# Transposing the attention output on TensorE in every unit, and storing the result in natural token order

## The chip, the core and the metric

The kernel runs on one NeuronCore of a Trainium2 chip. The metric is the device time in microseconds (us) of one execution, the median of repeated runs. Profile times are microseconds from the first instruction of the profiled execution.

## The reference

A gated linear attention with a decay per key channel, and after it a two-layer network with a squared relu. Inputs are float32; q, k, v and alpha are 4 batches x 8 heads x 768 tokens x 48 channels, the weights 384 x 2048 and 2048 x 384.

```python
state = zeros((B, H, D, D))
for t in range(S):
    state = alpha[:, :, t, :, None] * state + einsum('bhd,bhe->bhde', k[:, :, t], v[:, :, t])
    y[:, :, t] = einsum('bhd,bhde->bhe', q[:, :, t], state)
x = y.transpose(0, 2, 1, 3).reshape(B * S, H * D)      # 3072 x 384
h = x @ w_in
r = maximum(h, 0.0)
out = (r * r) @ w_out                                    # 3072 x 384, float32
```

## The kernel before

The 768 tokens of a batch are cut into three pieces of 256, so there are 12 units (g = 0 to 11), ordered piece by piece over the four batches. A unit goes through these steps, named here as the text below uses them, with the lines of the profile:

- **load** (L477): four transfers (alpha, k, q, v; 384 KB each) issued on SP's queue. Partition p holds the tokens 2p and 2p+1 of the unit, the two under an index j.
- **front**: the product of the two alphas (L493/L495), its logarithm (L496), cumulative sums on TensorE (L504 to L508, called m1), exponentials (L516 to L526), and scaled k and q in bf16 (`qks`, L542). Then q and k are transposed to `kqt`: on TensorE for units 0 to 2 (L556), and by a transposing transfer issued on SP's queue for units 3 to 11 (L569, one for k and one for q).
- **back**: the state update (L587, called kv), the scores (L625, one group of 16 matmuls into psX and one into psZ), the mask (L631), the attention output in psX (L645 and L652, called y), its copy to bf16 (`xbf`, L662 on ScalarE or L664 on VectorE). Then `xbf` is transposed to `xt`: for units 0 to 2 by six TensorE transposes into psX (L674) and a copy out (L680 or L682); for units 3 to 11 by a transposing transfer on SP's queue (L685).
- **moe**: the first layer in 8 groups of 6 matmuls (L712, called s1), each into one of two PSUM banks psH; a relu of each group to `rr` (L719 on ScalarE, L721 on VectorE) and a square to `gt` (L725, L728); the second layer as two tiles of 128 tokens with 16 matmuls each, cut into groups of 4 (L738, called s2), into the one bank psO; a copy out to `osb` (L745), and the store (L751).

Rows of `y` stand with j outside: partition 64j + s of half c is the token 2(64c + s) + j. That order goes through `xt`, `rr` and `gt` to the rows of `osb`, so each tile of 128 output rows is stored by two transfers of 64 rows, each to every second row of the output.

The order of every engine is fixed beforehand by a list scheduler in the kernel (`Program.schedule`): each operation has a cost in ns, a priority and dependencies, DMA transfers share the bandwidth by a table of weights, and the operation with the smallest priority among those that are ready goes next. Some operations have alternatives on other engines. The engines then run their lists strictly in that order and wait on semaphores; SP's list holds every load, every transposing transfer and every store. At the beginning, while TensorE has no work, matmuls on zeros are put in (L784).

Of the kernel before, what the change touches and what calls it, by code (L numbers as in the profile page):

```python
# [6 lines left out]
ALU = mybir.AluOpType  # L7
AF = mybir.ActivationFunctionType
# [25 lines left out]
class Program:  # L34
# [6 lines left out]
    RING = {"sp": 24.0, "act": 20.0, "pool": 130.0}  # L41
# [55 lines left out]
    def schedule(self):  # L97
# [9 lines left out]
        rings = {"sp": [], "act": [], "pool": []}  # L107
# [206 lines left out]
def act_ns(n):  # L314
    return 180 + n * 0.8333
# [10 lines left out]
def bass_gla_recurrent__then__act_relu_squared_kernel(  # L326
# [10 lines left out]
    HD = H * D  # L337
# [11 lines left out]
    PE_X = 3  # L349
# [110 lines left out]
    load_op = {}  # L460

# [3 lines left out]
    def load(g):  # L465
        b, i = units[g]
        t0 = i * T
        p0 = g * P
        r, la, qs, kt, pm, vb, x2 = (g % n for n in (NRAW, 2, NQKS, NKQT, NPM, NV, 2))
        first, last = i == 0, i == NST - 1  # L470
        xt = XSLOT[g]
        sr, sw = 2 * b + i % 2, 2 * b + (i + 1) % 2

        for j, t, nm in ((0, alpha, "a"), (1, k, "k"), (2, q, "q"), (3, v, "v")):
            src = t[b, :, t0:t0 + T, :].rearrange("h (p j) d -> p h (j d)", j=2)
            dst = RAW[r][:, j].rearrange("p h j d -> p h (j d)")
            load_op[g, nm] = add("sp", lambda e, dst=dst, src=src: e.dma_start(dst, src), 400, L_PRIO[g] + j,  # L477
                writes=[("raw", r, j)], name=f"ld{nm}{g}", dma=f"{nm}{r}", lag=1230,
                after=[load_op[AFTER[g]]] if g in AFTER else [])

    def front(g):
# [39 lines left out]
        if not last:  # L521
# [15 lines left out]
        vin, vout = RAW[r][:, 3].rearrange("p h j d -> p (h j d)"), VBF[vb][:].rearrange("p h j d -> p (h j d)")  # L537
        add("pool", lambda e: e.tensor_copy(vout, vin), 830, p0 + 900, reads=[("raw", r, 3)], writes=[("vbf", vb)],  # L538
            name=f"vc{g}", alts={"act": (lambda e: e.activation(vout, vin, AF.Copy), act_ns(2 * HD))})
# [8 lines left out]
        for a in range(2):  # L548
# [18 lines left out]
            else:  # L567
                dst = KQT[kt][:, a].rearrange("p j n s -> p (j n) s")
                add(TR_RING, lambda e, dst=dst, src=src: e.dma_start_transpose(dst, src), 500, p0 + 2500 + a,  # L569
                    reads=[("qks", qs, a)], writes=[("kqt", kt, a)], name=f"tr{a}_{g}", dma=f"t{a}_{kt}", lag=1250)  # L570

    def back(g):
# [111 lines left out]
        else:  # L684
            add(TR_RING, lambda e: e.dma_start_transpose(dst, src), 500, p0 + 6700, reads=[("xbf", x2)],  # L685
                writes=[("xt", s, slot)], name=f"xt{g}", dma=f"x{s}{slot}", lag=950)
# [5 lines left out]
    def moe(m, gs):  # L692
# [8 lines left out]
        for u in range(nb):  # L701
# [5 lines left out]
            def s1(pe, u=u, hb=hb):  # L707
# [11 lines left out]
            add("act", lambda e, hb=hb, rb=rb: e.activation(RR[rb][:], psH[hb][:], AF.Relu), act_ns(512), pu + 600,  # L719
                reads=[("ps", "H", hb)], writes=[("rr", rb)], name=f"re{m}_{u}",  # L720
                alts={"dve": (lambda e, hb=hb, rb=rb: e.tensor_scalar(RR[rb][:], psH[hb][:], 0.0, None, ALU.max),  # L721
# [7 lines left out]
        for ti, (ui, jq) in enumerate((ui, jq) for ui in range(nu_) for jq in range(2)):  # L729
# [18 lines left out]
            for j in range(2):  # L748
                r0 = b * S + i * T + 128 * jq + j
                dst = bass.AP(tensor=out.tensor, offset=out.offset + r0 * DM, ap=[[2 * DM, 64], [1, DM]])  # L750
                add("sp", lambda e, ob=ob, dst=dst, j=j: e.dma_start(dst, OSB[ob][64 * j:64 * j + 64, :]), 500,  # L751
                    ps_ + 1300, reads=[("osb", ob)], name=f"out{m}_{ti}_{j}", dma=f"o{ob}{j}", lag=300)
# [10 lines left out]
    for g in range(5, G):  # L763
# [3 lines left out]
             ("wout", 1): (2, "a"), 3: ("wout", 0), 4: ("wout", 0), 5: ("wout", 1), 6: ("wout", 1)}  # L767
# [48 lines left out]
```

## Time and profile before

| | |
|---|---|
| time, median of 3 runs (lowest to highest) | 194.6 us (194.4 to 195.27) |
| the profiled execution's own time | 195.71 us |
| its span, first to last instruction | 194.0 us |
| mean granted TensorE clock | 0.987 |
| busy: TensorE / weight loads / VectorE / ScalarE / GpSimd | 176.8 / 126.2 / 119.4 / 118.9 / 32.0 us |
| hardware DMA queue | 79,968 packets, 30.09 MB |

A row of the timeline gives the start, the length, the engine (PE is TensorE, DVE VectorE, ACT ScalarE, POOL GpSimd, SPq the queue of SyncE), the line, the operation with output<-input, and in brackets the idle time of that engine just ahead and what ended it. The chain of waits is followed back from the last instruction: start, length, what. The table of stretches gives for each stretch the busy time of the engines with their instruction counts, the granted clock of TensorE, the share of the DMA engines and GB/s.

### The profile page before, as it was taken

The numbers are of one execution on the slowest core, as the hardware profiler recorded it, in microseconds if no ns is written. First come the engines' busy times: TensorE is split into PE (matmuls) and PEld (weight loads), VectorE is DVE, ScalarE is ACT, GpSimd is POOL, SyncE is SP. The second block draws the span as 40 slices with busy tenths as digits, with TensorE's granted clock in tenths as the row PEclk, the third lists the DMA queues.
The fourth block names the chain that finished last, engine by engine and source line by source line (L and its number), as shares of the span: only waits on it lengthen the run. The fifth ranks groups of instructions, "written<-read, shape, count | busy, mean of one in ns | idle before, by whom it ended". The sixth has DMA issues, their size and how long they took to land.

```text
span 194.0 us, 5232 instructions
## 1 busy us (share of the span) xinstructions
PE 176.8 (91%) x2255; PEld 126.2 (65%) x2255; DVE 119.4 (62%) x204; ACT 118.9 (61%) x217; POOL 32.0 (16%) x40
## 2 busy tenths in 40 slices
PE   7998995999898949689999999999999999999980
PEld 5767883666574537357777668667777676677740
DVE  6698886676778738651983984929819427144210
ACT  3575796366768247916876768568757564466511
POOL 3061140105022324400300331301000101000000
PEclk9999999999999999969999999999999999999998
DMA  5999999989999999999899998562633440321211
GB/s 160 325 260 200 258 200 194 216 206 316 157 319 192 291 194 256 208 268 272 199 293 300 185 251 186 80 129 46 130 80 79 98 81 3 78 47 30 51 41 41
DMA packets 82870, 33.56 MB, mean 173 GB/s; under 512 B 76960, under 2 KB 82080, under 8 KB 82848
## 3 DMA queue, kind: packets, MB, share of 16 engines
q1 hardware_dynamic: 79968, 30.09, 68.7%
q0 software_dynamic: 2880, 3.15, 10.0%
q8 instruction: 17, 0.28, 0.6%
q14 instruction: 5, 0.04, 0.1%
HBM read 25.17 MB, written 4.72 MB: 154 GB/s over the span
## 4 chain that ended last, share of the span: by engine, by line
PE 62%; DMA 23%; ACT 4%; SPq 3%; DVE 2%; POOL 2%; issue 1%
PE psO L738 28%; PE psH L712 25%; DMA raw<-in_alpha_dram 12%; DMA wout<-in_moe_w_out_dram 5%; DMA win<-in_moe_w_in_dram 4%; DMA xt<-xbf 3%; PE psX L652 2%; PE psX L645 2%; PE psZ L587 2%; POOL prd L495 2%; SPq L477 2%; PE psX L625 1%; SPq L569 1%; PE psW L504 1%; PE psZ L625 1%
## 5 line engine op out<-in xcount | busy, mean ns | idle before, releaser
L712 PE MATMUL psH<-xt,win 128*128 128x256 bf16 x576 | 73.8, 274 | 5.7 <-DMA xt<-xbf 4.8
L738 PE MATMUL psO<-wout,gt 128*128 128x384 bf16 x384 | 73.1, 329 | 2.6 <-DMA wout<-in_moe_w_out_dram 2.1
L712 PEld LDWEIGHTS psH<-xt,win 128*128 128x128 bf16 x576 | 54.0, 98 | 18.0 <-DMA xt<-xbf 2.9
L719 ACT ACTIVATE rr<-psH 128x512 bf16<-128x512 f32 x84 | 49.9, 596 | 25.7 <-PE psH L712 24.1
L725 DVE TENSOR_TENSOR gt<-rr 128x512 bf16<-128x512 bf16 x66 | 28.8, 443 | 41.8 <-ACT rr L719 41.5
L738 PEld LDWEIGHTS psO<-wout,gt 128*128 128x128 bf16 x384 | 36.2, 98 | 23.3 <-DMA wout<-in_moe_w_out_dram 2.2
L745 ACT ACTIVATE osb<-psO 128x384 f32<-128x384 f32 x24 | 11.8, 491 | 22.7 <-PE psO L738 22.3
L728 ACT ACTIVATE gt<-rr 128x512 bf16<-128x512 bf16 x30 | 18.7, 626 | 1.3 <-DVE rr L721 0.8
L603 POOL TENSOR_TENSOR smd<-tmp,own 128x384 bf16<-128x384 f32 x7 | 7.4, 1057 | 56.2 <-DVE tmp L601 56.2
L631 DVE TENSOR_TENSOR pm<-psZ,caus 128x1024 bf16<-128x1024 f32 x12 | 14.6, 1217 | 1.7 <-PE psZ L625 1.7
L631 DVE TENSOR_TENSOR pm<-psX,caus 128x1024 bf16<-128x1024 f32 x12 | 14.6, 1217 | 0.9 <-PE psX L625 0.8
L721 DVE TENSOR_SCALAR rr<-psH 128x512 bf16<-128x512 f32 x12 | 8.3, 689 | 8.8 <-PE psH L712 8.7
L784 PE MATMUL psO<-zero 128*128 128x256 bf16 x77 | 12.0, 302 | 1.3 <-DVE zero L411 1.3
L662 ACT ACTIVATE xbf<-psX 128x768 bf16<-128x768 f32 x10 | 8.1, 810 | 6.9 <-PE psX L652 6.9
L542 DVE TENSOR_TENSOR qks<-raw,ek 128x768 bf16<-128x768 f32 x12 | 11.5, 955 | 0.4 <-POOL ek L528 0.2
L542 DVE TENSOR_TENSOR qks<-raw,eq 128x768 bf16<-128x768 f32 x12 | 11.4, 951 | 0.1
L496 ACT ACTIVATE lab<-prd 128x384 bf16<-128x384 f32 x12 | 6.2, 520 | 7.4 <-POOL prd L495 5.8
L784 PEld LDWEIGHTS psO<-zero 128*128 128x128 bf16 x77 | 8.0, 108 | 3.2 <-DVE zero L411 1.2
L610 POOL TENSOR_TENSOR sbd<-tmp,acm 128x384 bf16<-128x384 f32 x8 | 7.0, 870 | 18.0 <-DVE tmp L608 18.0
L495 POOL TENSOR_TENSOR prd<-raw 128x384 f32<-128x384 f32 x4 | 5.1, 1268 | 21.4 <-DMA raw<-in_alpha_dram 21.4
L538 POOL CAST vbf<-raw 128x768 bf16<-128x768 f32 x5 | 4.5, 891 | 21.4 <-DMA raw<-in_v_dram 17.7
L534 DVE TENSOR_TENSOR eq<-eq,raw 128x384 f32<-128x384 f32 x12 | 7.9, 657 | 0.0
(75 smaller groups left out, 145.8 us busy)
## 6 DMA issues: line engine op xcount, KB each, us to landing
raw<-in_alpha_dram SPq DMA_DIRECT2D x12, 384.0 KB, 3.9
raw<-in_k_dram SPq DMA_DIRECT2D x12, 384.0 KB, 4.4
raw<-in_q_dram SPq DMA_DIRECT2D x12, 384.0 KB, 5.0
raw<-in_v_dram SPq DMA_DIRECT2D x12, 384.0 KB, 5.2
out_dram<-osb SPq DMA_DIRECT2D x48, 96.0 KB, 2.3
win<-in_moe_w_in_dram POOLq DMA_DIRECT2D x2, 768.0 KB, 9.4
wout<-in_moe_w_out_dram POOLq DMA_DIRECT2D x2, 768.0 KB, 11.3
kqt<-qks SPq DMA_TRANSPOSE x18, 3.9
```

The lines of the kernel that those rows point to most:

```text
L495: alts={"pool": (lambda e: e.tensor_tensor(hd(PRD[la][:]), al(0), al(1), ALU.mult), pool_ns(HD))})
L542: add("dve", lambda e, a=a, E=E: e.tensor_tensor(QKS[qs][:, a, :, :, 0:D], RAW[r][:, 1 + a].rearrange("p h j d -> p j h d"), E[la][:].rear ...
L631: add("dve", lambda e, hf=hf, psT=psT: e.tensor_tensor(PM[pm][:, hf].rearrange("p r n j t -> p (r n) (j t)"), psT[:, :, :].rearrange("p r ...
L662: add("act", lambda e: e.activation(XBF[x2][:], psX[:, :, 0:HD], AF.Copy), act_ns(2 * HD), p0 + 6100, reads=[("ps", "X", 0), ("ps", "X", 1 ...
L712: ins = pe.matmul(psH[hb][:, i * n:(i + 1) * n], WIN[:, kk, fj * 128:(fj + 1) * 128], mov, start=(kk == 0), stop=(kk == KT - 1))
L719: add("act", lambda e, hb=hb, rb=rb: e.activation(RR[rb][:], psH[hb][:], AF.Relu), act_ns(512), pu + 600, reads=[("ps", "H", hb)], writes= ...
L721: alts={"dve": (lambda e, hb=hb, rb=rb: e.tensor_scalar(RR[rb][:], psH[hb][:], 0.0, None, ALU.max), dve_ns(512))})
L725: add("dve", lambda e, dst=dst, sq=sq: e.tensor_tensor(dst, sq, sq, ALU.mult), 415, pu + 1200, reads=[("rr", rb)], writes=[("gt", gt, g0 + ...
L728: "act": (lambda e, dst=dst, sq=sq: e.activation(dst, sq, AF.Square), act_ns(512))})
L738: ins = pe.matmul(psO[:, 0:DM], GT[gt][:, fj, g0 + ui, jq, :], WOUT[:, fj, :], start=(fj == 0), stop=(fj == FT - 1))
L745: add("act", lambda e, ob=ob: e.activation(OSB[ob][:], psO[:, 0:DM], AF.Copy), act_ns(DM), ps_ + 700, reads=[("ps", "O")], writes=[("osb", ...
L784: pr.fill(lambda pe: pe.matmul(psO[:, 0:256], ZERO[:, 0:128], ZERO[:, 0:256], skip_group_check=True), 109, min(o.start for o in pr.order[" ...
```

## The change

Four things are edited.

1. `PE_X` goes from 3 to the number of units: in all 12 units the six TensorE transposes into psX and a copy out make `xt`; the nine transposing transfers of L685 are gone.
2. The relu writes `rr` permuted: it reads psH as before and writes each element to its place with the token's j innermost, so consecutive elements of a run land 4 bytes apart. `rr`, `gt` and the output rows are then in natural token order.
3. The store of a tile is one transfer of 128 consecutive rows instead of two of 64.
4. The scheduler's description of the DMA is another: weights by kind of transfer in place of weights by queue, longer issue costs of transposing transfers and stores. Code for loads on another queue is added, with a constant that leaves all loads on SP (`SW_LOADS = G`), and entries of the table `AFTER` are taken out for units 4 to 6, which the next line of the code overwrites in both kernels.

```diff
-    RING = {"sp": 24.0, "act": 20.0, "pool": 130.0}
+    PACKET = (("win", 172), ("wout", 79), ("ld", 22), ("tr", 18), ("xt", 18), ("out", 65))
...
         def rates():
-            total = sum(self.RING[r] for r, q in rings.items() if q)
-            return {r: self.RING[r] / total for r, q in rings.items() if q}
+            took = {r: next(t for n, t in self.PACKET if q[0].name.startswith(n)) for r, q in rings.items() if q}
+            return {r: t / sum(took.values()) for r, t in took.items()}
...
-    PE_X = 3
+    PE_X = G
...
+    SW_LOADS = G
...
-                add(TR_RING, lambda e, dst=dst, src=src: e.dma_start_transpose(dst, src), 500, p0 + 2500 + a,
-                    reads=[("qks", qs, a)], writes=[("kqt", kt, a)], name=f"tr{a}_{g}", dma=f"t{a}_{kt}", lag=1250)
+                add(TR_RING, lambda e, dst=dst, src=src: e.dma_start_transpose(dst, src), 1300, p0 + 2500 + a,
+                    reads=[("qks", qs, a)], writes=[("kqt", kt, a)], name=f"tr{a}_{g}", dma=f"t{a}_{kt}", lag=1700)
...
-            add("act", lambda e, hb=hb, rb=rb: e.activation(RR[rb][:], psH[hb][:], AF.Relu), act_ns(512), pu + 600,
+            rin = psH[hb][:].rearrange("p (x j t) -> p x j t", j=2, t=64)
+            rout = RR[rb][:].rearrange("p (x t j) -> p x j t", j=2, t=64)
+            add("act", lambda e, rin=rin, rout=rout: e.activation(rout, rin, AF.Relu), act_ns(512), pu + 600,
...
-            for j in range(2):
-                r0 = b * S + i * T + 128 * jq + j
-                dst = bass.AP(tensor=out.tensor, offset=out.offset + r0 * DM, ap=[[2 * DM, 64], [1, DM]])
-                add("sp", lambda e, ob=ob, dst=dst, j=j: e.dma_start(dst, OSB[ob][64 * j:64 * j + 64, :]), 500,
-                    ps_ + 1300, reads=[("osb", ob)], name=f"out{m}_{ti}_{j}", dma=f"o{ob}{j}", lag=300)
+            r0 = b * S + i * T + 128 * jq
+            add("sp", lambda e, ob=ob, r0=r0: e.dma_start(out[r0:r0 + 128, :], OSB[ob][:]), 600, ps_ + 1300,
+                reads=[("osb", ob)], name=f"out{m}_{ti}", dma=f"o{ob}", lag=600)
```

With other operations and costs the scheduler writes other lists. On TensorE the two lists are the same, row for row but for one matmul on zeros, up to the first group of s1 matmuls ahead of unit 3's scores. The first place is the end of unit 4's back in the kernel before: the second group of scores of unit 4, its y, and the first s1 groups of unit 3.

```order
L625 MATMUL psZ<-kqt 64x128 x16
L738 MATMUL psO<-wout,gt 128x384 x4
L504 MATMUL psW<-lab,linc 128x384
L506 MATMUL psW<-hcol,hsel 128x8
L508 MATMUL psW<-ones,lab 128x2 x4
L645 MATMUL psX<-sbd,kqt 64x96 x8
L645 MATMUL psX<-smd,kqt 64x96 x8
L652 MATMUL psX<-vbf,pm 128x48 x32
L712 MATMUL psH<-xt,win 128x256 x12
```

In the changed kernel (line numbers are those of its own file: L651/L658 is y, L593 kv, L718 s1, L747 s2, L680 the transposes of `xbf`) unit 3's first s1 group is the last row here, before any score of unit 4:

```order
L651 MATMUL psX<-smd,kqt 64x96 x8
L658 MATMUL psX<-vbf,pm 128x48 x32
L593 MATMUL psZ<-vbf,qks 128x96 x16
L718 MATMUL psH<-xt,win 128x256 x6
L509 MATMUL psW<-lab,linc 128x384
L511 MATMUL psW<-hcol,hsel 128x8
L513 MATMUL psW<-ones,lab 128x2 x4
L680 MATMUL psX<-ident,xbf 128x128 x6
L747 MATMUL psO<-wout,gt 128x384 x4
L718 MATMUL psH<-xt,win 128x256 x6
```

So s1 of unit 3 has moved from behind y of unit 4 to a few groups behind y of unit 3; when unit 4's scores begin, three more s1 groups, two more s2 groups and one group of transposes have been issued than before. The transposes stand one or two groups behind y in the later units too. The second place is SP's list, from the loads of unit 6 on; before:

```order
L477 DMA raw<-in_v_dram 128x8x96
L685 DMA_TRANSPOSE xt<-xbf 128x6x128
L569 DMA_TRANSPOSE kqt<-qks 128x8x128
L751 DMA out_dram<-osb 64x384 x2
L569 DMA_TRANSPOSE kqt<-qks 128x8x128
L477 DMA raw<-in_alpha_dram 128x8x96
```

and in the changed kernel:

```order
L482 DMA raw<-in_v_dram 128x8x96
L575 DMA_TRANSPOSE kqt<-qks 128x8x128
L758 DMA out_dram<-osb 128x384
L575 DMA_TRANSPOSE kqt<-qks 128x8x128
L482 DMA raw<-in_alpha_dram 128x8x96
```

The transfer of `xbf` is gone from between the loads of unit 6 and the transposing transfers of unit 5, and the store is one row.

More of the change, by code (lines that the diff above doesn't have):

```diff
@@ L472, in load @@
         sr, sw = 2 * b + i % 2, 2 * b + (i + 1) % 2
+        ring, cost = ("sp", 600) if g < SW_LOADS else ("pool", 930)
         for j, t, nm in ((0, alpha, "a"), (1, k, "k"), (2, q, "q"), (3, v, "v")):
             src = t[b, :, t0:t0 + T, :].rearrange("h (p j) d -> p h (j d)", j=2)
-            dst = RAW[r][:, j].rearrange("p h j d -> p h (j d)")
-            load_op[g, nm] = add("sp", lambda e, dst=dst, src=src: e.dma_start(dst, src), 400, L_PRIO[g] + j,
-                writes=[("raw", r, j)], name=f"ld{nm}{g}", dma=f"{nm}{r}", lag=1230,
+            dst, key = RAW[r][:, j], ("raw", r, j)
+            if nm == "v" and ring == "pool":
+                dst, key = VBF[vb], ("vbf", vb)
+            dst = dst[:].rearrange("p h j d -> p h (j d)")
+            load_op[g, nm] = add(ring, lambda e, dst=dst, src=src: e.dma_start(dst, src), cost, L_PRIO[g] + j,
+                writes=[key], name=f"ld{nm}{g}", dma=f"{nm}{r}{ring}", lag=1230,
                 after=[load_op[AFTER[g]]] if g in AFTER else [])
@@ L684, in back @@
         else:
-            add(TR_RING, lambda e: e.dma_start_transpose(dst, src), 500, p0 + 6700, reads=[("xbf", x2)],
-                writes=[("xt", s, slot)], name=f"xt{g}", dma=f"x{s}{slot}", lag=950)
+            add(TR_RING, lambda e: e.dma_start_transpose(dst, src), 1300, p0 + 6700, reads=[("xbf", x2)],
+                writes=[("xt", s, slot)], name=f"xt{g}", dma=f"x{s}{slot}", lag=1400)
     rr_i = [0]
```

11 lines of the change are left out of this document (6 added, 5 removed).

## The prediction

> **What bounds the kernel now.** First the table of stretches (after the span and its length: TensorE, weight loads, VectorE, ScalarE, GpSimd, then the granted clock, the DMA share and GB/s).
>
> ```profile
> 50.00:60.00 10.00, 9.11 (x135) 6.68 (x134) 8.06 (x11) 7.34 (x15) 2.00 (x2) 1.00 1.22 262
> 60.00:70.00 10.00, 7.13 (x128) 4.06 (x126) 7.30 (x11) 5.14 (x11) 2.54 (x3) 1.00 1.12 237
> 70.00:80.00 10.00, 8.41 (x107) 6.24 (x108) 6.11 (x10) 6.38 (x12) 3.45 (x4) 1.00 0.99 246
> 80.00:90.00 10.00, 7.96 (x89) 5.13 (x88) 3.45 (x5) 4.48 (x10) 1.81 (x2) 0.83 1.13 244
> ...
> 100.00:180.00 80.00, 79.97 (x1005) 57.52 (x1004) 47.09 (x78) 51.19 (x91) 8.24 (x8) 1.00 0.56 116
> ```
>
> From 100 to 180 TensorE has no gap: whatever it does there, it does back to back, and only less work or an earlier start can end it sooner. Between 50 and 90 it is idle 0.89 + 2.87 + 1.59 + 2.04 = 7.4 us, and in the last ten of these the clock was granted at 0.83. So the question is what ends the gaps there. TensorE's own timeline names it:
>
> ```profile
> 53.29 0.42 PE L625 MATMUL psX<-kqt 64*64 64x128 bf16 x16 [0.76 <-DMA kqt<-qks]
> ...
> 63.36 0.42 PE L625 MATMUL psX<-kqt 64*64 64x128 bf16 x16 [1.26 <-DMA kqt<-qks]
> ...
> 71.36 1.48 PE L712 MATMUL psH<-xt,win 128*128 128x256 bf16 x12 [2.81 <-DMA xt<-xbf]
> ...
> 82.95 1.39 PE L712 MATMUL psH<-xt,win 128*128 128x256 bf16 x6 [2.04 <-DMA xt<-xbf]
> ```
>
> The two long ones are s1 of units 3 and 4, waiting for the transposing transfer that the change removes. The two short ones are scores waiting for transfers that stay. Why `xt` is late stands in VectorE's row for `xbf` of unit 3 and in SP's timeline:
>
> ```profile
> 58.10 0.95 DVE L664 CAST xbf<-psX 128x768 bf16<-128x768 f32 x1
> ```
>
> ```profile
> 51.38 0.58 SPq L477 DMA_DIRECT2D raw<-in_alpha_dram  x1
> ...
> 59.51 1.85 SPq L569 DMA_TRANSPOSE kqt<-qks  x1
> 61.41 0.58 SPq L477 DMA_DIRECT2D raw<-in_alpha_dram  x1
> ...
> 65.46 2.06 SPq L685 DMA_TRANSPOSE xt<-xbf  x1
> 67.57 1.31 SPq L569 DMA_TRANSPOSE kqt<-qks  x1
> ...
> 70.76 1.36 SPq L569 DMA_TRANSPOSE kqt<-qks  x1
> ```
>
> `xbf` is ready at 59.05, but its transfer is issued at 65.46, behind the transposing transfer of unit 4 and the four loads of unit 6 on SP, and lands just before 71.36: 12.3 us, of which 6.4 are queueing.
>
> **The change part by part.** Prices at full clock come from the chain of waits, where TensorE runs without gaps:
>
> ```profile
> 43.21 0.34 PE psX L674 x6
> ...
> 90.95 0.16 PE psW L504
> 91.12 0.45 PE psZ L587 x16
> ...
> 92.98 0.65 PE psO L738 x4
> 93.63 1.31 PE psH L712 x12
> ...
> 96.89 0.35 PE psX L625 x16
> 97.24 0.22 PE psZ L625 x16
> ...
> 100.84 0.46 PE psX L645 x16
> 101.30 0.51 PE psX L652 x32
> ```
>
> *How much can be won at all.* From 53.29 to 82.95 are 29.66 us. The list of the kernel before has in them 78 s1 matmuls (6.5 x 1.31 = 8.5), 44 of s2 (11 x 0.65 = 7.15), three units' scores (3 x 0.57 = 1.7), two y (one without its state half: 1.8), two kv (0.9) and the m1 parts (five of 0.16 and their small matmuls, about 1.1): 21.2 us. The same count over the gapless stretch from 89.64 to 186.04 falls 4% short of its 96.4 us, so 0.85 of the missing 8.5 us is the price of any stretch; 7.6 are lost. Ahead of 53.29 come 0.76. Behind 82.95 the clock is still low:
>
> ```profile
> 82.95 1.39 PE psH L712 x6
> 84.34 1.28 PE psO L738 x4
> 85.62 0.78 PE psX L645 x16
> ```
>
> This is 3.45 us for what costs 0.655 + 0.65 + 0.46 = 1.77: 1.7 lost. In all 10.1 us is the ceiling of the gain.
>
> *Does it go?* In the changed list `xt` of unit 3 is made right behind its y. With `xbf` at about 59, transposes 0.34 and the copy out, s1 of unit 3 is free at about 60.5 instead of 71.3. Ahead of unit 4's scores the list now has three s1 groups (1.96), two s2 groups (1.3) and the transposes (0.34): 3.6 us of work, against the 1.26 us in which these scores waited, while the transfers they wait for are issued no later (59.51 for the second). Unit 3's scores get one s1 and one s2 group more ahead of them, 1.3 us for a wait of 0.76, and begin at about 53.8. Behind them TensorE has 3.5 us of s1, s2 and m1 to do while VectorE masks unit 4. So both `xt` waits and both `kqt` waits have cover. If it fails, unit 4's scores wait at most their old 1.26 us. Next in line are unit 5's scores: their two transfers were issued at 67.57 and 70.76; without the 2.06 us of `xt` ahead of them and with one store issue less they go out by about 65.5 and 68.5, land by 72.5 (the median below), and the list needs them at 53.8 + 20.9 = 74.7, with 19.6 us of work and 1.3 us for its ends between. From there each unit costs TensorE about 13.6 us, against 10.0 us from the alpha load of unit 5 (51.38) to that of unit 6 (61.41) on SP, so loads no longer come last. Small waits for the logarithm (about 0.5 in sum) stay. I take -9.6 us, bounds -4.9 (the two idle times alone) and -10.1.
>
> The clock's loss is in this sum only because it follows a gap. The Trainium skill's page TensorE: Matmul & The Clock Gate (What's actually happening) has the clock halve after an idle window of some 3.4 us that runs freely. The trace agrees in part: 2.04 us of idle ending at 82.95 brought 0.83, yet the 2.81 us ending at 71.36 left 1.00.
>
> ```profile
> out_dram<-osb SPq DMA_DIRECT2D x48, 96.0 KB, 2.3
> ...
> kqt<-qks SPq DMA_TRANSPOSE x18, 3.9
> ```
>
> *Transposes.* Nine units x 0.34 = +3.1 us, on the engine that sets the end. Each waits for `xbf`, and the next unit's scores wait for psX. The durations:
>
> ```profile
> L719 ACT ACTIVATE rr<-psH 128x512 bf16<-128x512 f32 x84 | 49.9, 596 | 25.7 <-PE psH L712 24.1
> ...
> L721 DVE TENSOR_SCALAR rr<-psH 128x512 bf16<-128x512 f32 x12 | 8.3, 689 | 8.8 <-PE psH L712 8.7
> ...
> L662 ACT ACTIVATE xbf<-psX 128x768 bf16<-128x768 f32 x10 | 8.1, 810 | 6.9 <-PE psX L652 6.9
> ...
> L496 ACT ACTIVATE lab<-prd 128x384 bf16<-128x384 f32 x12 | 6.2, 520 | 7.4 <-POOL prd L495 5.8 <-DVE prd L493 1.5
> ...
> L674 PE MATMUL psX<-ident,xbf 128*128 128x128 bf16 x18 | 1.5, 219 | 0.0
> ...
> L680 DVE COPY xt<-psX 128x768 bf16<-128x768 bf16 x2 | 1.1, 552 | 0.2 <-PE psX L674 0.2
> ```
>
> Behind y stand one or two s1 groups (0.66 to 1.31 us) before the transposes, `xbf` takes 0.81 to 0.95: the wait is 0 to 0.4 us a unit, so 0 to +3.6; the nearest row, where three units do this already with no idle ahead of the matmuls (0.0), says near zero: +0.3. The nine copies out (9 x 0.55 on VectorE, 0.81 at the pace of `xbf` on ScalarE, 5 to 7 us) lie beside the s1 groups of the same unit, on engines that are busy 47.09 and 51.19 of 80 us; without that cover they would cost their own time.
>
> *The relu.* Same input, same count, each result written 4 bytes from the last. No row shows such a write. Below: 0 (a gain is excluded, the same elements pass). Above: every element at double time, 512 x 0.84 ns (from 810 and 596 ns at 768 and 512) = +0.43 us each. The nearest row is `lab` (L496), which writes 48-element runs with gaps: 520 ns for 384 elements, where 596 - 128 x 0.84 = 488 would be the plain price. I take 0.
>
> The Trainium skill, Advanced Engine Details and Errata (SBUF Cachelines), wants two hits per 16-byte line; 4 bytes apart gives four, so by it 0 too. Its VectorE Performance Modes ask unit step for the doubled rate, which speaks against the permuted write; by that the relu on VectorE loses only if it had it, and at 689 ns, 1.35 a element, it has not.
>
> *Stores.* 24 issues fewer and nine transfers fewer: SP is relieved by 24 x 0.59 + 9 x 1.29 = 26 us.
>
> ```profile
> L751 SPq DMA_DIRECT2D out_dram<-osb x48: 466/594/1409, 40.4 to 190.4; - x48
> L685 SPq DMA_TRANSPOSE xt<-xbf x9: 1210/1294/2063, 65.5 to 167.6; - x9
> 189.42 0.49 ACT osb L745
> ```
>
> Where TensorE is gapless this is worth nothing. At the end it is: after the last copy (189.42 + 0.49) two issues go out one after the other, now one. -0.6 for the issue, up to +1.0 for the landing of 96 KB more (96 KB land in 2.3 us, the transposing transfers of 256 KB in 3.9: 1.6 / 160 x 96): 0 between them.
>
> Sum: -9.6 + 3.1 + 0.3 + 0 + 0 = **-6.2 us**. The profiled execution, 195.71 us with a span of 194.0, becomes 189.5; the median shown is 1.1 lower, 194.6, and becomes **188.4**.
>
> **The rivals.** *The wait moves to SP.* The queue is serial, and `kqt` and the loads stay on it; the DMA share is 0.99 to 1.22 in all the stretches to 90. Then the `kqt` waits and the low clock stay, and only 4.85 us of `xt` waits go: -4.85 + 3.1 = -1.8, **192.8**. Against it: SP's items are fewer, and the list has 3.6 us in front of the wait.
>
> *The relu's write is slow, and the kernel gets slower.* Its place is the two psH banks: TensorE fills one in 0.655 us, and a relu of 1.03 us does not empty it as fast. In the changed list six s1 groups stand in a row around each transpose group; 6 x 0.375 - 0.34 = 1.9 us a unit, for units 4 to 11 15 us: 188.4 + 15 = **203**. It decides from the point where 8 x (6x - 0.34) reaches 6.2, a relu of about 0.84 us. For it: no row shows the write. Against it: `lab`'s row.
>
> *The freed time is not filled.* Later units start no earlier, because another chain (alpha, product, logarithm, m1) sets their pace, and TensorE pays 3.1 us: about **197**. For it: in the kernel before the alpha loads come 10 us apart through this stretch, and little lies between their landing and m1. Against it: from 100 on the same chain feeds units of 13.6 us and nothing waits.
>
> **How the numbers follow.** Forecast 0.67, in its own range 186 to 190.5. Wait moves to SP 0.17 (190.5 to 193.7). Slow relu 0.08; time not filled 0.08, one case in four of it within the band. The low end of the range is the ceiling with nothing new, -10.1 + 3.1 - 0.6 = -7.6, 187.0, less 1.5 for loads that come earlier than counted: 185.5. The high end holds the first rival's 192.8 and 0.7 more: 193.5. About 1 in 6 is left out. A difference of 0.5%, 1 us, is about what can be told from no change: faster 0.67 + 0.15 = 0.82, same 0.05, slower 0.13.
>
> **What would show it.** Right: TensorE's stretches from 60 to 90 above 9.5 of 10 with the clock at 1.00; s1 of unit 3 at 60 to 61 with no wait for `xt`; nine more groups of six transposes at 0.34 us; TensorE's last matmul at 182 to 184 instead of 189.4; relu at 596 and 689 ns. Wrong: relu means above 0.65 us with TensorE waiting for psH; gaps ended by `kqt` or alpha of 1 us or more between 60 and 90; transposes each with a wait of 0.5 us for `xbf`.

## The result

The changed kernel takes 187.44 us (median of 4 runs, 186.87 to 188.21), beside 194.5 us for the kernel before in the same comparison: a ratio of 0.963, interval 0.959 to 0.968. The profiled execution took 187.19 us with a span of 185.5 us and a mean clock of 1.00. Some executions of a kernel are of a slower kind; medians, ratios and intervals from here on are of the others alone, which leaves two executions of T undone, too few for an interval, and N alone without a profile that times can be read from.

The table of stretches of the changed kernel, with the columns of the prediction:

```profile
50.00:60.00 10.00, 9.79 (x159) 7.29 (x157) 8.99 (x14) 8.06 (x15) 1.82 (x2) 1.00 1.14 250
60.00:70.00 10.00, 10.00 (x149) 7.45 (x148) 9.10 (x13) 7.84 (x16) 3.30 (x3) 1.00 1.20 279
70.00:80.00 10.00, 10.00 (x148) 6.75 (x148) 8.02 (x12) 6.41 (x11) 1.86 (x2) 1.00 1.21 257
80.00:90.00 10.00, 10.00 (x131) 7.53 (x124) 7.89 (x14) 8.59 (x18) 1.83 (x2) 1.00 1.09 297
...
100.00:180.00 80.00, 79.24 (x973) 56.99 (x972) 46.81 (x80) 51.03 (x83) 8.10 (x8) 1.00 0.35 77
```

TensorE has no gap between 60 and 100 and the clock stays at 1.00. Its timeline at the places where it stood before (scores and s1 of unit 3, scores of units 4 and 5):

```profile
52.47 0.42 PE L631 MATMUL psX<-kqt 64*64 64x128 bf16 x16
...
57.87 0.49 PE L680 MATMUL psX<-ident,xbf 128*128 128x128 bf16 x6
59.22 0.83 PE L718 MATMUL psH<-xt,win 128*128 128x256 bf16 x6 [0.21 <-DVE xt L686]
...
63.53 0.42 PE L631 MATMUL psX<-kqt 64*64 64x128 bf16 x16
...
73.11 0.42 PE L631 MATMUL psX<-kqt 64*64 64x128 bf16 x16
```

All four waits are gone; of the one for `xt` 0.21 us is left. In SP's timeline the loads of units 6, 7 and 8 begin (with the one for alpha) here:

```profile
57.68 0.66 SPq L482 DMA_DIRECT2D raw<-in_alpha_dram  x1
...
66.43 1.07 SPq L482 DMA_DIRECT2D raw<-in_alpha_dram  x1
...
75.36 0.58 SPq L482 DMA_DIRECT2D raw<-in_alpha_dram  x1
```

They are 9 us apart. Before, the alpha of unit 6 was issued at 61.41. The durations, the store, and the last copy out:

```profile
L728 ACT ACTIVATE rr<-psH 128x512 bf16<-128x512 f32 x84 | 60.2, 746 | 19.5 <-PE psH L718 19.3
...
L730 DVE TENSOR_SCALAR rr<-psH 128x512 bf16<-128x512 f32 x12 | 8.8, 735 | 2.2 <-PE psH L718 2.2
L680 PE MATMUL psX<-ident,xbf 128*128 128x128 bf16 x72 | 6.0, 219 | 0.0
L686 DVE COPY xt<-psX 128x768 bf16<-128x768 bf16 x10 | 5.5, 553 | 6.2 <-PE psX L680 6.2
L688 ACT ACTIVATE xt<-psX 128x768 bf16<-128x768 bf16 x2 | 1.6, 802 | 0.0
```

```profile
out_dram<-osb SPq DMA_DIRECT2D x24, 192.0 KB, 2.8
```

```profile
L758 SPq DMA_DIRECT2D out_dram<-osb x24: 332/396/1326, 39.1 to 182.5; - x24
```

```profile
182.01 0.49 ACT L754 ACTIVATE osb<-psO 128x384 f32<-128x384 f32 x1 [2.87 <-PE psO L747]
```

The permuted relu takes 746 ns on ScalarE where the plain one took 596, and 735 on VectorE where it took 689. The transposes wait for nothing (0.0). One store issue has a median of 396 ns, against 594 ns for each of two. After the last copy the kernel ends in 185.5 - 182.5 = 3.0 us; before it was 194.0 - 189.91 = 4.1 us.

So the 8.5 us between the two profiled executions are: 7.4 us by which the last copy ends earlier, and 1.1 us at the tail. The 7.4 us are, from TensorE's idle time and prices: 7.2 us less idle between 50 and 110 us (7.39 to 0.21), 1.95 us less idle in the first 50 us (4.60 to 2.65, a wait for the weights at the start, which comes and goes from kernel to kernel: 2.5 to 4.6 us in all those below), some 1.7 us of the low clock, and +3.1 us for nine more groups of transposes: -7.7 us.

### The profile page after: what moved, and what is told of

It reads as the page before. It is cut to its first block, busy times and chain, and to the rows that moved or that the text cites. A ratio compares the mean times of both kernels' runs of the same rounds, so it can differ in the third digit from the quotient of the medians.

```text
span 185.5 us, 5311 instructions
## 1 busy us (share of the span) xinstructions
PE 178.4 (96%) x2310; PEld 128.5 (69%) x2310; DVE 126.7 (68%) x218; ACT 125.6 (68%) x214; POOL 29.9 (16%) x38
## 4 chain that ended last, share of the span: by engine, by line
PE 77%; DMA 15%; DVE 2%; SPq 2%; ACT 1%; issue 1%
PE psO L747 34%; PE psH L718 30%; DMA raw<-in_alpha_dram 6%; DMA wout<-in_moe_w_out_dram 5%; DMA win<-in_moe_w_in_dram 5%; PE psX L658 3%; PE psX L651 2%; PE psZ L593 2%; PE psX L631 2%; SPq L482 2%; PE psX L680 2%; PE psZ L631 2%; PE psW L509 1%; ACT rr L728 1%; DVE pm L637 1%
## 5 line engine op out<-in xcount | busy, mean ns | idle before, releaser
L718 PE MATMUL psH<-xt,win 128*128 128x256 bf16 x576 | 73.1, 273 | 1.4 <-DMA win<-in_moe_w_in_dram 0.8
L728 ACT ACTIVATE rr<-psH 128x512 bf16<-128x512 f32 x84 | 60.2, 746 | 19.5 <-PE psH L718 19.3
L747 PE MATMUL psO<-wout,gt 128*128 128x384 bf16 x384 | 71.4, 326 | 0.7 <-ACT osb L754 0.6
L718 PEld LDWEIGHTS psH<-xt,win 128*128 128x128 bf16 x576 | 53.0, 98 | 13.4 <-ACT rr L728 1.5
L747 PEld LDWEIGHTS psO<-wout,gt 128*128 128x128 bf16 x384 | 36.0, 98 | 22.1 <-ACT osb L754 1.0
L734 DVE TENSOR_TENSOR gt<-rr 128x512 bf16<-128x512 bf16 x69 | 30.3, 444 | 28.5 <-ACT rr L728 27.9
L737 ACT ACTIVATE gt<-rr 128x512 bf16<-128x512 bf16 x27 | 16.6, 628 | 1.3 <-DVE rr L730 0.8
L609 POOL TENSOR_TENSOR smd<-tmp,own 128x384 bf16<-128x384 f32 x6 | 6.3, 1042 | 60.5 <-DVE tmp L607 60.5
L535 DVE TENSOR_TENSOR ek<-ek,raw 128x384 f32<-128x384 f32 x11 | 7.2, 652 | 4.7 <-ACT ek L521 4.7
L668 ACT ACTIVATE xbf<-psX 128x768 bf16<-128x768 f32 x9 | 7.3, 811 | 4.2 <-PE psX L658 4.2
L686 DVE COPY xt<-psX 128x768 bf16<-128x768 bf16 x10 | 5.5, 553 | 6.2 <-PE psX L680 6.2
```

Of the source, the lines that this page charges most:

```text
L718: ins = pe.matmul(psH[hb][:, i * n:(i + 1) * n], WIN[:, kk, fj * 128:(fj + 1) * 128], mov, start=(kk == 0), stop=(kk == KT - 1))
L728: add("act", lambda e, rin=rin, rout=rout: e.activation(rout, rin, AF.Relu), act_ns(512), pu + 600, reads=[("ps", "H", hb)], writes=[("rr" ...
L734: add("dve", lambda e, dst=dst, sq=sq: e.tensor_tensor(dst, sq, sq, ALU.mult), 415, pu + 1200, reads=[("rr", rb)], writes=[("gt", gt, g0 + ...
L737: "act": (lambda e, dst=dst, sq=sq: e.activation(dst, sq, AF.Square), act_ns(512))})
L747: ins = pe.matmul(psO[:, 0:DM], GT[gt][:, fj, g0 + ui, jq, :], WOUT[:, fj, :], start=(fj == 0), stop=(fj == FT - 1))
```

## Experiments

The change has three parts that can be had one by one: **T**, all units transposed by TensorE; **N**, the permuted relu with one store of 128 rows; **M**, the scheduler's new description of the DMA. In each kernel the scheduler writes its lists anew, so most edits come with the order that follows from them, and then the run cannot tell the two apart. Some pairs are free of this: in their traces every engine runs the same operations in the same order, matmuls on zeros and the number of stores aside. These are the kernel before, N, and N with two stores; T + M and the same with the longer relu; and the change and the one that is permuted in the copy. T and T + N differ only in the place of one relu on VectorE and in one product that goes from GpSimd to VectorE.

This is what was measured. M holds the new table of weights and longer issue costs of loads and transposing transfers; the longer cost of the one store goes with N. Beside each group of runs the kernel before was run again, with medians of 194.5 to 195.0 us; a ratio is to the kernel before in its own group, so it is not always the quotient of two rows of the first column. The last two columns are from the profiled execution of each.

| kernel | median us | ratio to the kernel before | interval | TensorE idle, 50 to 110 us | from the last copy to the end, us |
|---|---|---|---|---|---|
| before | 194.5 | 1 | | 7.39 | 4.1 |
| T | 195.7 | 1.004 | 0.999 to 1.009 | 8.55 | 3.8 |
| M | 194.59 | 0.998 | 0.994 to 1.002 | 6.91 | 4.1 |
| N | 188.78 | 0.971 | 0.964 to 0.979 | | |
| T + N (M undone) | 193.11 | 0.988 | 0.983 to 0.993 | 2.47 | 3.0 |
| M + N (T undone) | 191.13, 188.49 | 0.966 to 0.980 | none | 5.61 | 3.2 |
| T + M (N undone) | 191.61 | 0.984 | 0.976 to 0.991 | 3.56 | 3.9 |
| T + M + N (the change) | 187.44 | 0.963 | 0.959 to 0.968 | 0.21 | 3.0 |
| N, two stores of 64 rows | 196.49 | 1.009 | 1.003 to 1.014 | 7.50 | 4.0 |
| T, stores by GpSimd | 194.98 | 1.001 | 0.996 to 1.006 | 4.14 | 5.9 |
| T + M, stores by GpSimd | 192.09 | 0.987 | 0.980 to 0.994 | 1.38 | 5.9 |
| T + M, relu of 1024 | 197.98 | 1.017 | 1.010 to 1.023 | 2.88 | 3.8 |
| change, permuted in the copy | 188.36 | 0.967 | 0.962 to 0.972 | 0.66 | 2.9 |
| change, 7 units by TensorE | 186.66 | 0.956 | 0.951 to 0.962 | 0.59 | 3.2 |

### One part alone

T alone, `PE_X = G` in the kernel before:

```diff
-    PE_X = 3
+    PE_X = G
```

> The kernel before with one edit: all 12 units make xt with TensorE transposes; relu, stores and the scheduler's DMA description stay. Theory A (the xt waits carried the time): both xt waits and the low clock go, TensorE pays 9 x 0.34; ratio to the kernel before 0.965 to 0.975 (187.7 to 189.6 us). Theory B (the scheduler's new DMA description makes the gain): 0.99 to 1.01. Theory C (SP's relief by fewer store issues makes it): 0.98 to 0.99, since 9 transfers of 35 go from SP.

It measured 1.004. The waits for `xt` are gone, and others stand in their place: 2.5 us for `gt`, 2.2 for `kqt`, 2.2 for `rr`, 1.2 for the mask and 0.4 for `lab`. TensorE's, ScalarE's, VectorE's and SP's timelines of T alone:

```profile
73.01 0.83 PE L712 MATMUL psH<-xt,win 128*128 128x256 bf16 x6 [2.19 <-ACT rr L719]
93.07 0.82 PE L738 MATMUL psO<-wout,gt 128*128 128x384 bf16 x4 [2.11 <-DVE gt L725]
```

```profile
70.84 0.84 ACT L539 ACTIVATE vbf<-raw 128x768 bf16<-128x768 f32 x1 [4.81 <-DMA raw<-in_v_dram]
```

```profile
91.52 0.56 DVE L493 TENSOR_TENSOR prd<-raw 128x384 f32<-128x384 f32 x1 [3.39 <-DMA raw<-in_alpha_dram]
```

```profile
86.98 0.59 SPq L477 DMA_DIRECT2D raw<-in_alpha_dram  x1
```

TensorE waits at 73.01 for a relu that ScalarE could not begin, because ahead of it in ScalarE's list stands the cast of a v that lands only at 70.84. At 93.07 it waits for a square; VectorE had stood 3.39 us in front of the product of alphas, whose load was issued at 86.98. TensorE's idle time is not less than before (8.55 us), and it has the transposes to do on top. This is close to the prediction's third rival, with the loads as the chain that sets the pace. SP's rows show that taking the nine transfers out of its list did not bring the loads of the next two units forward. The alphas of units 6 and 7 in T:

```profile
61.64 0.58 SPq L477 DMA_DIRECT2D raw<-in_alpha_dram  x1
...
71.56 0.59 SPq L477 DMA_DIRECT2D raw<-in_alpha_dram  x1
```

In the kernel before they went out at 61.41 and 72.16. Those of units 8 and 9 are some 5 us earlier than there (77.75 and 86.98 against 82.51 and 92.24), and VectorE still stands 3.39 us in front of the last of them.

M alone is the new table of weights and the new issue costs in the kernel before:

```diff
-    RING = {"sp": 24.0, "act": 20.0, "pool": 130.0}
+    PACKET = (("win", 172), ("wout", 79), ("ld", 22), ("tr", 18), ("xt", 18), ("out", 65))
```

> The kernel before with one edit: the scheduler's weights by kind of transfer and its longer issue costs; the nine transposing transfers, the relu and the two stores a tile stay. Theory A: the xt of units 3 and 4 still lands about 12 us after xbf, so TensorE still waits 3 to 6 us between 55 and 90: ratio 0.99 to 1.01. Theory B: 0.965 to 0.975. Theory C: 0.99 to 1.01.

It measured 0.998: nothing. N alone is the permuted relu and the one store in the kernel before:

```diff
-            add("act", lambda e, hb=hb, rb=rb: e.activation(RR[rb][:], psH[hb][:], AF.Relu), act_ns(512), pu + 600,
+            add("act", lambda e, rin=rin, rout=rout: e.activation(rout, rin, AF.Relu), act_ns(512), pu + 600,
...
-                add("sp", lambda e, ob=ob, dst=dst, j=j: e.dma_start(dst, OSB[ob][64 * j:64 * j + 64, :]), 500,
+            add("sp", lambda e, ob=ob, r0=r0: e.dma_start(out[r0:r0 + 128, :], OSB[ob][:]), 600, ps_ + 1300,
```

> The kernel before with one edit: the permuted relu write and one store of 128 rows a tile; the transposing transfers and the scheduler's description stay. Theory A: the end gets 0.5 to 1.1 us shorter, the relu takes 0.75 us on ScalarE without TensorE waiting for it, the xt waits stay: ratio 0.985 to 1.0. Theory B: 0.99 to 1.0. Theory C: most of the gain, 0.965 to 0.98.

It measured 0.971, the only gain of a part alone and most of the gain of the whole change (0.963; the intervals overlap between 0.964 and 0.968), although the transposing transfers are all still there and every list is that of the kernel before.

### One part undone

T undone leaves `PE_X = 3` in the changed kernel:

```diff
-    PE_X = G
+    PE_X = 3
```

> The changed kernel with one edit undone: units 3 to 11 make xt by a transposing transfer again; relu, store and scheduler's description as changed. Theory A: the gain goes but for the end's 1 us: ratio to the kernel before 0.985 to 1.0. Theory B: the gain stays, 0.96 to 0.97. Theory C: 0.97 to 0.98.

Two executions, 191.13 and 188.49 us; in the first, which is the profiled one, TensorE is idle for 5.61 us between 50 and 110. What T is worth on top of M + N lies between nothing and 3 us, and these runs don't settle it. M undone is T and N with the old table:

```diff
-    PACKET = (("win", 172), ("wout", 79), ("ld", 22), ("tr", 18), ("xt", 18), ("out", 65))
+    RING = {"sp": 24.0, "act": 20.0, "pool": 130.0}
```

> All transposes on TensorE, permuted relu and one store a tile; the scheduler's old description of the DMA (weights by queue, short issue costs). Theory S: SP has both reliefs, so the loads come in time whatever the scheduler believes: ratio to the kernel before 0.96 to 0.97. Theory M (the scheduler's description is the third part of the gain, since the list that it makes with the old one lets engines sit in front of late loads): 0.975 to 0.99.

0.988, which is worse than N alone: with the old costs T takes some 3 us (1.6%) from what N gives. Beside T alone it shows what the 24 issues do at nearly the same lists: 1.004 becomes 0.988, TensorE's idle time goes from 8.55 to 2.47 us, and the alphas of units 6 and 7 go out 2.7 and 3.5 us earlier than in T:

```profile
58.93 1.35 SPq L477 DMA_DIRECT2D raw<-in_alpha_dram  x1
...
68.08 1.20 SPq L477 DMA_DIRECT2D raw<-in_alpha_dram  x1
```

Its one long gap is again of the kind that T alone showed: TensorE waits 2.04 us at 90.06 for a square while VectorE has stood 3.11 us for an alpha that was issued at 84.62; in the changed kernel the alpha of that unit goes out at 82.37. N undone is the changed kernel with the plain relu and two stores:

```diff
-            rout = RR[rb][:].rearrange("p (x t j) -> p x j t", j=2, t=64)
-            add("act", lambda e, rin=rin, rout=rout: e.activation(rout, rin, AF.Relu), act_ns(512), pu + 600,
+            add("act", lambda e, hb=hb, rb=rb: e.activation(RR[rb][:], psH[hb][:], AF.Relu), act_ns(512), pu + 600,
...
-            add("sp", lambda e, ob=ob, r0=r0: e.dma_start(out[r0:r0 + 128, :], OSB[ob][:]), 600, ps_ + 1300,
+                add("sp", lambda e, ob=ob, dst=dst, j=j: e.dma_start(dst, OSB[ob][64 * j:64 * j + 64, :]), 500,
```

> The changed kernel with the old relu and the two stores of 64 rows: transposes on TensorE and the scheduler's new description alone. Theory S: SP keeps its 48 store issues, loads come late, in-order lists of ScalarE and VectorE stand before them: ratio to the kernel before 0.985 to 1.0. Theory of the prediction (the xt waits carry it, given a list that has work in front of the other waits): 0.965 to 0.975.

0.984, with 3.56 us of idle time. Here the way from SP's list to TensorE can be read row by row: SP, then VectorE, ScalarE and TensorE.

```profile
71.57 0.58 SPq L482 DMA_DIRECT2D raw<-in_alpha_dram  x1
...
75.52 1.80 SPq L758 DMA_DIRECT2D out_dram<-osb  x2
77.36 1.75 SPq L575 DMA_TRANSPOSE kqt<-qks  x1
79.16 0.59 SPq L758 DMA_DIRECT2D out_dram<-osb  x1
79.80 0.59 SPq L482 DMA_DIRECT2D raw<-in_alpha_dram  x1
```

```profile
75.56 0.56 DVE L498 TENSOR_TENSOR prd<-raw 128x384 f32<-128x384 f32 x1 [2.39 <-DMA raw<-in_alpha_dram]
...
83.98 0.56 DVE L498 TENSOR_TENSOR prd<-raw 128x384 f32<-128x384 f32 x1 [1.83 <-DMA raw<-in_alpha_dram]
84.45 0.42 DVE L732 TENSOR_TENSOR gt<-rr 128x512 bf16<-128x512 bf16 x1
84.79 0.95 DVE L670 CAST xbf<-psX 128x768 bf16<-128x768 f32 x1
```

```profile
76.15 0.52 ACT L501 ACTIVATE lab<-prd 128x384 bf16<-128x384 f32 x1 [3.06 <-DVE prd L498]
76.58 0.47 ACT L752 ACTIVATE osb<-psO 128x384 f32<-128x384 f32 x1
```

```profile
77.11 2.77 PE L745 MATMUL psO<-wout,gt 128*128 128x384 bf16 x16 [1.36 <-ACT osb L752]
...
85.80 0.51 PE L680 MATMUL psX<-ident,xbf 128*128 128x128 bf16 x6 [1.34 <-DVE xbf L670]
```

SP issues the alpha of unit 7 at 71.57, it lands 4 us later, and VectorE stands in front of the product until 75.56. ScalarE stands behind it in the logarithm until 76.15, with the copy that empties psO next in its list, and for this copy TensorE waits 1.36 us. The alpha of unit 8, issued at 79.80 behind three stores and a transposing transfer, does the same to `xbf`, and TensorE waits 1.34 us for that. In the changed kernel unit 8's alpha goes out at 75.36, and neither wait is there.

### The count of the stores, or SP

N alone again, but stored by two transfers of 64 consecutive rows, so that with the same lists only the count of store issues (and with it the rows of each) differs from N:

```diff
-            add("sp", lambda e, ob=ob, r0=r0: e.dma_start(out[r0:r0 + 128, :], OSB[ob][:]), 600, ps_ + 1300,
+            for j in range(2):
+                add("sp", lambda e, ob=ob, r0=r0, j=j: e.dma_start(out[r0:r0 + 64, :], OSB[ob][64 * j:64 * j + 64, :]), 500,
```

> The kernel before with the permuted relu and natural token order, but each tile stored by two transfers of 64 consecutive rows, so SP issues 48 stores as before. Theory S (SP's serial list is late, and fewer store issues bring loads and transposing transfers forward): most of what the one store won is gone, ratio to the kernel before 0.985 to 1.0. Theory D (the order of the rows in memory makes the stores cheaper for the DMA engines, whatever their number): 0.965 to 0.98, as with one store.

1.009: the whole gain of N is gone, and what is left of N (the permuted relu and the other order of rows) costs a little. So the gain of N is in the 24 issues, not in the order of the rows or of the operations. Then the stores were taken from SP altogether, and issued by GpSimd in the old two halves, once with T and once with T and M:

```diff
-                add("sp", lambda e, ob=ob, dst=dst, j=j: e.dma_start(dst, OSB[ob][64 * j:64 * j + 64, :]), 500,
+                add("pool", lambda e, ob=ob, dst=dst, j=j: e.dma_start(dst, OSB[ob][64 * j:64 * j + 64, :]), 1000,
```

> The kernel with only the transposes moved to TensorE, and the 48 stores of 64 rows issued by GpSimd in place of SP; the relu, the rows' order and the DMA's bytes are as before. Theory S: SP is relieved of 48 issues, so the gain appears: ratio to the kernel before 0.965 to 0.98, with alpha loads of units 6 to 9 issued 2 to 6 us earlier than with the transposes alone. If the DMA engines' bandwidth is the bound and not SP's list: 0.995 to 1.01.

> The changed kernel with the plain relu and two stores of 64 rows for each tile, as in the run with those two undone (191.6 us), but all 48 stores issued by GpSimd and none by SP. Theory A, the store part of the change pays by freeing SP's serial queue (24 issues of 0.594 us): 187 to 189 us, since now SP has 48 issues less, with the waits of 1.36 and 1.34 us between 75 and 90 us gone. Theory B, it pays by something else (the number of store transfers, the tail of one issue, GpSimd's own order being disturbed): 190.5 to 193 us, and TensorE keeps gaps of 1 us or more between 60 and 90 us.

By the time alone both look as if SP had nothing to do with it: 1.001 and 0.987, where T gave 1.004 and T + M 0.984. The profiles say otherwise. T + M with the stores on GpSimd (stretch from 50 to 110, then GpSimd and ScalarE at the end):

```profile
50.00:110.00 60.00, 58.62 (x816) 41.82 (x815) 45.30 (x67) 43.77 (x84) 25.14 (x32) 1.00 1.16 264
```

```profile
183.88 0.49 ACT L752 ACTIVATE osb<-psO 128x384 f32<-128x384 f32 x1 [2.87 <-PE psO L745]
184.66 1.04 POOL L758 DMA_DIRECT2D out_dram<-osb  x2 [2.31 <-ACT osb L752]
```

TensorE's idle time falls from 3.56 to 1.38 us, and with T alone from 8.55 to 4.14; the last copy ends 2.3 us earlier than in T + M with the stores on SP (184.37 against 186.64). But with its stores on GpSimd the kernel ends 5.9 us after the last copy, where SP's two issues need 3.9, and 2.0 us of the gain are lost there. The time of both is the one that the rival theory gave (0.995 to 1.01, and 190.5 to 193 us), but the loads moved as theories S and A said. When SP issued the alpha of each unit, in us:

| kernel | unit 6 | unit 7 | unit 8 | unit 9 |
|---|---|---|---|---|
| before | 61.41 | 72.16 | 82.51 | 92.24 |
| T | 61.64 | 71.56 | 77.75 | 86.98 |
| T + N | 58.93 | 68.08 | 74.96 | 84.62 |
| T, stores by GpSimd | 59.26 | 66.50 | 74.64 | 83.36 |
| T + M | 61.31 | 71.57 | 79.80 | 88.30 |
| T + M, stores by GpSimd | 58.87 | 67.08 | 74.55 | 83.39 |
| the change | 57.68 | 66.43 | 75.36 | 82.37 |

With the stores off SP they go out 2.4 to 5.3 us earlier, and more than half of TensorE's idle time between 50 and 110 is gone, though not all of it. The bytes to be moved are the same, and the DMA engines move them faster in that stretch: 258 GB/s against 243 with T, 264 against 247 with T + M. So the DMA engines were not at their limit. At the end GpSimd's stores give the gain back. The 0.3 us that should be left are less than the medians can tell. How much of SP's lateness is the cost of issues and how much its order is not separated here: in T + M its rows fill 37.6 of the 40 us from 50 to 90, but about 7.3 us of that are its own waits ahead of transposing transfers, by the releasers that the profile infers. And moving the stores changed the lists as well.

### The relu

T + M (N undone) with a ScalarE relu of 1024 elements:

```diff
-            add("act", lambda e, hb=hb, rb=rb: e.activation(RR[rb][:], psH[hb][:], AF.Relu), act_ns(512), pu + 600,
+            add("act", lambda e, hb=hb, rb=rb: e.activation(RR[rb][:].rearrange("p (r n) -> p r n", r=2), twice(psH[hb][:]), AF.Relu), act_ns(512), pu + 600,
```

> The changed kernel with the relu and the two stores of the kernel before (the run with those two undone, 191.6 us), and ScalarE's relu reading its 512 elements twice into a tile of 1024, so that its duration is about 1.02 us (596 + 512 x 0.84); the answer is the same. Slow-relu rival of the prediction, with its point of 0.84 us: the two psH banks cannot be emptied as fast as TensorE fills them in 0.655 us each, so TensorE waits for relu about 6 x 0.365 - 0.34 = 1.85 us in each of eight units or more, some 15 us: 205 to 208 us, with rr as the largest releaser of TensorE's s1 waits. Theory that the relu has cover far beyond the 0.84 us, because VectorE takes part of the relus and s2, scores and y stand between the s1 groups: 191 to 194 us.

197.98 us: between the two. Against T + M the ratio is 1.0166 / 0.9838 = 1.033, some 6.4 us. Groups of the longer relu, and who waited for `rr` (us, times):

```profile
L729 ACT ACTIVATE rr<-psH 128x1024 bf16<-128x1024 f32 x87 | 86.1, 1027 | 11.8 <-PE psH L721 11.8
```

```profile
  PEld psH L721: 10.4, 29
```

TensorE's weight loads of s1 wait for the relu at 29 places, 10.4 us in all, against 3 places and 0.8 us in T + M; the lists are the same. The rival's mechanism is there, at less than half of its price. Then the permutation was taken out of the relu of the changed kernel and put into the copy of the transposes:

```diff
-            add("dve", lambda e: e.tensor_copy(dst.rearrange("p a t -> p (a t)"), bank[:, 0:768]), dve_ns(768, 2),
+            xin = bank[:, 0:768].rearrange("p (a j t) -> p a j t", j=2, t=64)
+            xout = dst.rearrange("p a (t j) -> p a j t", j=2)
+            add("dve", lambda e: e.tensor_copy(xout, xin), dve_ns(768, 2),
```

> The changed kernel with the permutation moved from the 96 relus to the 12 copies of the transposes out of PSUM; the relu is the plain one of the kernel before, the one store of 128 rows stays. Theory A, the permuted bf16 write costs 25% wherever it stands: relu back at 596 and 689 ns, the 12 copies longer by about a quarter (553 to 690 ns on VectorE, some 1.6 us in all in place of 12 to 13 us on ScalarE), TensorE no longer waits for relu; since TensorE is gapless, time 186.5 to 187.5, ratio to the changed kernel 0.995 to 1.000. Theory B, the relu of 746 ns holds TensorE at several places: 184 to 186.5 us.

```profile
L728 ACT ACTIVATE rr<-psH 128x512 bf16<-128x512 f32 x84 | 50.0, 596 | 25.2 <-PE psH L720 23.7
...
L688 DVE COPY xt<-psX 128x768 bf16<-128x768 bf16 x10 | 10.2, 1018 | 6.3 <-PE psX L680 6.3
...
L690 ACT ACTIVATE xt<-psX 128x768 bf16<-128x768 bf16 x2 | 2.0, 1025 | 0.0
```

The relu is back at 596 ns, and ScalarE is relieved of 10.2 us. The copy on VectorE is not a quarter longer, as expected, but 84% (1018 ns against 553); the two on ScalarE are 28% longer (1025 against 802). The time is 0.967, and the interval overlaps that of the change, so theory B falls, and theory A's small gain was not seen either. The run takes 150 ns from each relu and adds 465 to each copy on VectorE, so by itself it shows only that the two together are worth nothing that can be measured. That the relu's 150 ns were hidden is seen in the waits: the weight loads of s1 waited for it 1.7 us at 5 places in the changed kernel and 0.8 us at 3 here.

### The price of the transposes

The changed kernel with TensorE's transposes in units 0 to 6, and transposing transfers again in units 7 to 11:

```diff
-    PE_X = G
+    PE_X = 7
```

> The changed kernel with TensorE's transposes in units 0 to 6 only; units 7 to 11 go back to the transposing transfer (five more on SP). Theory A, the price of 0.34 us a unit is fully paid where TensorE has no gap, and after 100 us the transfer lies ready in time: 5 x 0.34 = 1.7 us less, 185.5 to 186 us, ratio to the kernel before 0.954 to 0.957. Theory B, the SP queue with its loads of units 8 to 11 behind the transfers makes new waits for xt between 85 and 125 us of 1 to 2 us each: 187.5 to 190 us.

0.956, against 0.963 for the change. The intervals overlap, so the medians do not settle whether this kernel is the faster one; if it is, by about 0.7%. TensorE's transposes and the stretch from 50 to 110 in its profile:

```profile
L680 PE MATMUL psX<-ident,xbf 128*128 128x128 bf16 x42 | 3.5, 219 | 0.0
```

```profile
50.00:110.00 60.00, 59.41 (x851) 43.00 (x849) 48.64 (x74) 46.88 (x84) 13.48 (x14) 1.00 1.12 265
```

No new wait came for `xt`, so theory B falls. From these two executions the price can be worked out: in the first 50 us TensorE was busy 46.28 us here and 47.35 in the changed kernel, so it was 1.07 us behind at 50, and its last copy ends 0.68 us ahead (181.82 against 182.50): 1.75 us won, for five groups of 0.34 us (1.7). Between 50 and 110 it lost 0.38 us to more idle time (0.59 against 0.21); without that it would be 2.1 us, or 0.43 a group. It is one execution of each.

## Why the prediction was right, and where it was not

The forecast was 188.4 us and the time is 187.44. Its sum stands up better than its reasons.

**What bounds the kernel** was read rightly: gaps of TensorE between 50 and 90, and none behind. **The gain of 9.6 us** was the right size: 7.2 us of idle time and 1.7 us of low clock in that stretch are 8.9. The start, 1.95 us less idle, was in no term; it seems to belong to the one execution, and the medians, which differ by 7.1 us, are near 7.2 + 1.7 + 1.1 - 3.1 = 6.9 without it.

**The step that failed** is the reason given for this term: that with `xt` made on TensorE and the new list ahead of the `kqt` waits the gaps close and "loads no longer come last", while the stores add nothing. T + M is the kernel nearest to that reasoning, and it leaves 3.56 us of idle time and a ratio of 0.984. What held TensorE was SP's list as a whole, and without the `xt` transfers the loads of the units behind were still late: T alone leaves 8.55 us, and in T and in T + M the alphas of units 6 and 7 go out within 0.6 us of the kernel before. That the term came out at the right size is luck in so far as the stores, put at nothing, closed what the transposes left open. With the loads late, the engines that take them in order stand in front of them, and what stands behind in their lists (a relu, a square, a copy out of psO, `xbf`) reaches TensorE late. The third rival (0.08) is close to what T alone does; that the loads no longer come last, which the prediction held already true, needed the other two parts. Only all three together end the gaps: idle 8.55 with T, 3.56 with T + M, 2.47 with T + N, 5.61 with M + N, 0.21 with all. In time it goes further against the step: N alone, which leaves the nine transfers on SP, has most of the gain, and T beside it gains only where M comes too, by an amount (0 to 3 us) that the runs leave open. How N alone closes the `xt` waits is not shown by any profile.

**The stores** were put at 0, with the sentence that SP's relief is worth nothing where TensorE is gapless. That was true behind 100 us, and the wrong place to look: between 50 and 100 it was not gapless, and there the 24 issues decide. Undoing N in the changed kernel costs from 0.963 to 0.984, about 4 us, with other lists; in the kernel before, with the same lists, one issue in place of two takes 1.009 to 0.971, and about 1 us of that is the tail (4.0 us with two stores, 3.0 in T + N). At the end the tail is 1.1 us shorter, outside the bounds of -0.6 to +0.4.

**The scheduler's new costs** were priced nowhere in the prediction, which took the lists as they came. M alone is worth nothing, but with T and N it is 0.988 to 0.963, over 4 us; on T + N it takes the idle time from 2.47 to 0.21. It acts through the lists alone (the order, and which engine takes an operation), and which moves in them do it was not separated.

**The relu** was taken at no extra time, and has 150 ns more on ScalarE and 46 on VectorE, inside the bounds of 0 to 0.43 us. Its 0.746 us are above the 0.65 us that the prediction named as a sign of being wrong, but TensorE hardly waited for it. By the rival's formula such a relu would have cost 8 x (6 x 0.091 - 0.34) = 1.6 us; the run that takes it back to 0.596 us, and lengthens the copies, is not faster. The rival's price was too high at the other point too: it took six s1 groups in a row to wait at each pair of banks, 15 us at 1.03 us; the run with 1.027 us lost 6.4 us. So the change would only about break even with a relu of that length.

**The transposes** at 0.34 us a unit are borne out by the run with five fewer (0.34 to 0.43 in one execution of each), and their waits for `xbf`, put at 0.3 us, were 0.0.

On the Trainium skill: its page Advanced Engine Details and Errata (SBUF Cachelines) would have left a write at 4 bytes' distance at full rate; the measured rise from 596 to 746 ns on ScalarE does not agree, and the measurement decides. The same page of the Trainium skill, in VectorE Performance Modes, asks unit step for the doubled rate; the copy of `xt` on VectorE agrees, with 0.72 ns an element written in a row (553 ns) and 1.33 permuted (1018 ns).

## What to carry to other kernels

Where one queue issues every load, transfer and store in a fixed order, price a change by all that stands in that queue: a removed issue is worth the earlier start of the next load, and it is seen on engines that never touch the queue, as a relu or a copy behind a product that stood for its input. When a wait that ends last is removed, look at once for the next thing that comes from the same queue; here removing nine of the transfers alone gained nothing, and halving the stores did, at an unchanged order. And a permutation has to be paid in some write: look for the engine that has room for it, and compare the totals. Here these are 84 relus with 150 ns more on ScalarE and 12 with 46 on VectorE, 13.2 us, against 10 copies with 465 ns more on VectorE and two with 223 on ScalarE, 5.1 us. The time was the same either way.

## What was not expected of the hardware

- A bf16 write with 4 bytes between consecutive elements costs ScalarE about 0.29 ns an element, in the relu (150 ns for 512) and in the two copies of `xt` that it made (1025 against 802 ns for 768) alike; VectorE 0.09 ns in the relu from f32 (46 ns for 512) and 0.61 in the copy of bf16 (465 ns for 768).
- One store of 128 consecutive rows is issued in 396 ns (median) on SP in the changed kernel, one of 64 rows in 594 in the kernel before and in N with two stores, whatever the order of the rows. All 24 together take 13.1 us of SP's time, the 48 took 31.4. Between 50 and 90 us, where it counts here, one issue of either size takes 0.8 us on average.
- A kernel whose last stores were issued by GpSimd ended 5.9 us after the last copy in both runs, one whose stores were issued by SP after 2.9 to 4.1 us.
